# Three matrix products share one step: the expert's second product moves to the step's head

## Chip, cores, metric

One core of a Trainium2 chip. The metric is the device time of one execution in microseconds (us), lower is better.

## What is computed

An FFT convolution, then a routed expert layer, then a dense layer with softplus. Cut to what matters here (3072 tokens of 256 channels go to each batch, 8 batches, 8 experts with a capacity of 768 tokens each; tokens that no expert keeps are zero):

```python
y   = irfft(rfft(x, axis=1) * F, axis=1)          # tokens, 256 channels
e   = argmax(y @ w_gate)                          # one expert for each token
h   = relu(disp[e] @ w1[e])                       # 256 -> 1024
m   = gate * (h @ w2[e])                          # 1024 -> 256
hin = m @ w_in                                    # 256 -> 2048
g   = max(hin, 0) + log1p(exp(-abs(hin)))         # softplus
out = g @ w_out                                   # 2048 -> 256
```

Both factors of each of the four large products are split into a high and a low part, and three of the four partial products are summed.

## The kernel before

The work behind the convolution is cut into 16 **units** of 384 tokens of one expert (the list `units`; 8 experts by two blocks of slots). A unit goes through four products on PE, each in groups of matmuls that a method of `Unit` issues:

- `w1(j)`, j from 0 to 7 (line 542): 6 matmuls into a PSUM tile `pw`, then ACT's relu `hh` and DVE's remainder `hl`.
- `w2(j)`, j from 0 to 7 (line 559): 6 matmuls into the two PSUM tiles `py`, summed over all j. After the eighth, ACT copies `yh` and DVE makes `yl`.
- `wi(i)`, i from 0 to 15 (line 574), the product with w_in: 6 matmuls into a PSUM tile `pi`. `sp_act` follows on ACT (`ab` twice, then `ln`, lines 469, 470, 472), `sp_sum` on DVE (`g`, line 477), and two steps later `sp_split` (ACT's `gh`, POOL's `gl`, lines 394 and 395).
- `wo(i)` (line 597), the product with w_out: 9 matmuls into three PSUM tiles `po`, summed over all i.

When a unit's sixteenth `wo` is done, `take` (line 604) copies its three `po` tiles to `ot` on DVE, and three stores on POOL (line 609) write them out. `tr_x` (line 531) turns a unit's tokens by transposes on PE into a tile `pt`. Weights of experts come by DMA as `ws`, and `split_w` makes `w1h`, `w2h` on ACT and `w1l`, `w2l` on POOL.

PSUM tiles come from pools that go round: `psa` has three buffers, and `pi`, `pw` and `pt` take the next one in turn; `psy` has two, both for the `py` of one unit; `pso` has three, all for the `po` of one unit. A tile that takes a buffer waits until the last reader of the tile before in it is done: a `pi` waits for the `g`, `hl` or `xl` that read its buffer last, and the first `wo` of a unit for the `take` of the unit before.

The order of all instructions is written by hand (a manual schedule, every engine in program order). Each call is entered by `ev(t, rank, ...)` at a step t, and `step(t)` issues the calls of one step sorted by rank, so the ranks say who comes first within a step:

```python
WI, SP, WO, SUM, W2, W1, TAKE, TR, AHEAD = range(9)
```

Unit v has its `wi` in steps 16v to 16v + 15, its `wo` four steps after each, and its `take` in step 16v + 19. From the third unit on, with b = 16(v - 2):

```python
ev(b + 2 * j - 3 if v > 1 else 8 * v - 19 + j, W1, u.w1, j)
ev(b + 2 * j if v > 1 else 8 * v - 16 + j, W2, u.w2, j)
```

So an even step from 0 to 222 has `wi`, `wo`, `w2`; an odd one to 219 has `wi`, `wo`, `w1`. The last steps have `wi` and `wo` alone. Transposes (`tr_x`, rank TR) stand at the end of the odd steps b - 7 and b - 5. Steps before 0 belong to the convolution and to the first two units' `w1` and `w2`, and no `wi` is in them. In steps up to 19 the conversion of w_in and w_out (`split_res`, lines 449 to 465, on DVE and ACT) still runs. From step 50 on come the first stores, with those of units 0, 1 and 2 in steps 50, 52 and 54, while `late_scatter` (line 815, POOL) goes on to step 67.

Of the kernel before, what the change touches and what calls it, by code (L numbers as in the profile page):

```python
# [95 lines left out]
def body(tc, cap, x, ff, fx, wg, w1, w2, win, wout, m1, m2, m4, small, out):  # L96
# [552 lines left out]
    with tc.manual_schedule():  # L649
# [53 lines left out]
                fn(*args)  # L703

        units = [Unit(e, r + e * UNIT) for r in [hi, *range(0, hi, region)] for e in range(E)]
        WI, SP, WO, SUM, W2, W1, TAKE, TR, AHEAD = range(9)
        T1, T2, S2, GG, S4, GATE, S3, X1, ON = range(-9, 0)


# [277 lines left out]
```

## Time and profile before

| | |
|---|---|
| median of three runs | 1119.17 us (1118.44 to 1120.66) |
| the profiled execution's own time | 1115.93 us |
| its span, first to last instruction | 1114.1 us |
| mean granted TensorE clock | 0.987 of full speed |
| PE busy (matmuls) | 1056.2 us, 95% |
| PEld busy (weight loads) | 1000.0 us, 90% |
| ACT, POOL, DVE busy | 828.5, 597.2, 502.3 us |

The profile is of one execution. PE is TensorE's matmuls and PEld its weight loads, which run beside them; DVE is VectorE, ACT ScalarE, POOL GpSimd. A matmul's shown duration overlaps with the next one's, so what a matmul costs is read from one start to the next. A row names a line of the kernel, the tile written, `<-`, the tiles read. Brackets at a row's end give the idle time before it and what ended that.

### The profile page before, as it was taken

How to read it: one execution, taken by the hardware profiler on the slowest of the kernel's cores; microseconds unless marked ns; L12 is line 12 of the kernel's file. 1: busy time of each engine (PE TensorE's matmuls, PEld its weight loads, DVE VectorE, ACT ScalarE, POOL GpSimd, SP SyncE). 2: the span in 40 equal slices, each digit the busy share in tenths (PEclk: the TensorE clock that was granted, in tenths of full speed). 3: DMA queues.
4: the chain of work that ended last, by engine and by line, in shares of the span. 5: the costliest groups of instructions: out<-in, count | busy, mean ns of one | idle time of the engine just before them, and what ended most of it. 6: DMA issues, size and time to landing. Idle time of an engine off the chain costs nothing.

```text
span 1114.1 us, 19249 instructions
## 1 busy us (share of the span) xinstructions
PE 1056.2 (95%) x7040; PEld 1000.0 (90%) x7040; DVE 502.3 (45%) x1001; ACT 828.5 (74%) x1689; POOL 597.2 (54%) x590
## 2 busy tenths in 40 slices
PE   9989999778889999999999999999999999999996
PEld 7978877468778999999999999999999999999996
DVE  3757586388998743323233333333323333232221
ACT  5547665555878787777888787878877877777884
POOL 1313837534446566786554655555555555554554
PEclk9999999979999999999999999999999999999999
DMA  9942403765533156444332333332112111100000
GB/s 276 284 116 66 113 23 85 195 165 168 153 99 96 55 179 225 139 139 131 106 126 76 132 105 115 110 105 85 53 53 62 53 53 55 60 11 6 16 15 18
DMA packets 102777, 114.88 MB, mean 103 GB/s; under 512 B 12397, under 2 KB 89666, under 8 KB 102673
## 3 DMA queue, kind: packets, MB, share of 16 engines
q1 hardware_dynamic: 95760, 100.90, 30.5%
q0 software_dynamic: 6912, 12.65, 3.6%
q8 instruction: 57, 0.93, 0.4%
q14 instruction: 48, 0.39, 0.1%
HBM read 66.20 MB, written 50.48 MB: 105 GB/s over the span
## 4 chain that ended last, share of the span: by engine, by line
PE 79%; DVE 9%; DMA 3%; issue 3%; POOL 2%; ACT 2%; SPq 0%; POOLq 0%; DVEq 0%; ACTq 0%
PE po L597 23%; PE pi L574 23%; PE py L559 10%; PE pw L542 10%; PE p L204 3%; PE p L286 3%; PE p L221 2%; PE p L244 2%; DMA disp<-yt,ix 1%; PE p L251 1%; DVE wr L451 1%; PE p L211 1%; DVE whb L459 1%; DVE wtop L461 1%; DVE g L477 1%
## 5 line engine op out<-in xcount | busy, mean ns | idle before, releaser
L395 POOL TENSOR_TENSOR gl<-g,gh 128x384 fp32r<-128x384 f32 x256 | 260.7, 1019 | 190.9 <-ACT gh L394 161.2
L477 DVE SCALAR_TENSOR_TENSOR g<-pi,ln 128x384 f32<-128x384 f32 x256 | 142.5, 557 | 463.6 <-ACT ln L472 454.8
L597 PE MATMUL po<-woh,gh 128*128 128x256 f32 x768 | 218.0, 284 | 8.9 <-ACT ab L469 7.9
L597 PE MATMUL po<-woh,gl 128*128 128x256 f32 x768 | 216.9, 282 | 1.0 <-POOL gl L395 1.0
L597 PE MATMUL po<-wol,gh 128*128 128x256 f32 x768 | 216.7, 282 | 0.0
L469 ACT ACTIVATE ab<-pi 128x384 f32<-128x384 f32 x256 | 125.8, 491 | 83.1 <-PE pi L574 69.4
L574 PE MATMUL pi<-yh,wih 128*128 128x384 f32 x512 | 175.8, 343 | 9.5 <-DVE g L477 9.4
L574 PE MATMUL pi<-yh,wil 128*128 128x384 f32 x512 | 173.0, 338 | 0.0
L574 PE MATMUL pi<-yl,wih 128*128 128x384 f32 x512 | 172.5, 337 | 0.0
L597 PEld LDWEIGHTS po<-woh,gh 128*128 128x128 f32 x768 | 144.9, 189 | 14.5 <-ACT ab L469 12.0
L597 PEld LDWEIGHTS po<-woh,gl 128*128 128x128 f32 x768 | 145.3, 189 | 1.3 <-POOL gl L395 1.3
L597 PEld LDWEIGHTS po<-wol,gh 128*128 128x128 f32 x768 | 145.5, 189 | 0.0
L470 ACT ACTIVATE ab<-ab 128x384 f32<-128x384 f32 (+1 forms) x257 | 134.9, 525 | 8.1
L472 ACT ACTIVATE ln<-ab 128x384 f32<-128x384 f32 (+1 forms) x257 | 134.8, 525 | 8.1
L395 POOL TENSOR_TENSOR w1l<-ws,w1h 128x512 fp32r<-128x512 f32 x64 | 84.0, 1312 | 94.8 <-ACT w1h L394 91.6
L395 POOL TENSOR_TENSOR w2l<-ws,w2h 128x512 fp32r<-128x512 f32 x64 | 84.2, 1316 | 88.6 <-ACT w2h L394 59.7
L394 ACT CAST gh<-g 128x384 fp32r<-128x384 f32 x256 | 129.7, 507 | 0.3 <-DVE g L477 0.3
L546 ACT ACTIVATE hh<-pw 128x384 fp32r<-128x384 f32 x128 | 62.7, 490 | 71.9 <-PE pw L542 71.9
L574 PEld LDWEIGHTS pi<-yh,wih 128*128 128x128 f32 x512 | 96.6, 189 | 15.3 <-DVE g L477 12.0
L574 PEld LDWEIGHTS pi<-yl,wih 128*128 128x128 f32 x512 | 96.7, 189 | 0.0
L574 PEld LDWEIGHTS pi<-yh,wil 128*128 128x128 f32 x512 | 96.5, 188 | 0.0
L542 PE MATMUL pw<-xl,w1h 128*128 128x384 f32 x256 | 88.6, 346 | 4.0 <-DVE xl L533 4.0
(139 smaller groups left out, 2062.9 us busy)
## 6 DMA issues: line engine op xcount, KB each, us to landing
ws<-in_w_dram SPq DMA_DIRECT2D x128, 256.0 KB, 3.0
out_dram<-cr SPq DMA_DIRECT2D x48, 512.0 KB, 3.9
xt<-in_x_dram SPq DMA_DIRECT2D x20, 384.0 KB, 4.2
disp<-pf SPq DMA_DIRECT2D x12, 516.0 KB, 8.8
xd<-disp SPq DMA_DIRECT2D x48, 129.0 KB, 3.1
wst<-in_win_dram SPq DMA_DIRECT2D x16, 256.0 KB, 4.4
wst<-in_wout_dram SPq DMA_DIRECT2D x16, 256.0 KB, 3.0
lt<-parked SPq DMA_DIRECT2D x32, 96.8 KB, 2.0
```

Of the source, the lines that this page charges most:

```text
L204: nc.tensor.matmul(ps[:, i], lhsT=xt[:, 4 * (g % 2) + i], rhs=self.m1s, start=True, stop=True)
L394: nc.scalar.copy(dst_hi, src)
L395: nc.gpsimd.tensor_tensor(out=dst_lo, in0=src, in1=dst_hi.bitcast(F32), op=ALU.subtract)
L469: nc.scalar.activation(out=ab[:, :n], in_=h, func=ACTF.Abs)
L470: nc.scalar.activation(out=ab[:, :n], in_=ab[:, :n], func=ACTF.Exp, scale=-1.0)
L472: nc.scalar.activation(out=ln[:, :n], in_=ab[:, :n], func=ACTF.Ln, bias=1.0)
L477: nc.vector.scalar_tensor_tensor(out=g[:, :n], in0=h, scalar=0.0, in1=ln[:, :n], op0=ALU.max, op1=ALU.add)
L542: nc.tensor.matmul(ps, lhsT=a[:, k, fs], rhs=b[:, k], start=(n == 0), stop=(n == 5))
L546: nc.scalar.activation(out=hh, in_=ps, func=ACTF.Relu)
L559: nc.tensor.matmul(self.py[d], lhsT=a[:, j % 2, ds], rhs=b, start=(j == 0 and n == 0), stop=(j == 7 and n == 2))
L574: nc.tensor.matmul(self.pi, lhsT=a[i][:, k], rhs=b[:, k], start=(n == 0), stop=(n == 5))
L597: nc.tensor.matmul(self.po[t], lhsT=a[:, ts], rhs=b[:, i], start=(i == 0 and n == 0), stop=(i == KI - 1 and n == 2))
```

## The change

The order of the ranks: W2 goes from the fifth place to the first. Nothing is added or taken away.

```diff
-        WI, SP, WO, SUM, W2, W1, TAKE, TR, AHEAD = range(9)
+        W2, WI, SP, WO, SUM, W1, TAKE, TR, AHEAD = range(9)
```

The calls of the convolution have negative ranks and stand ahead of both. In steps before 0 there is nothing of rank WI to SUM, so the order there stays as it was.

PE around the change of a unit, from the last matmul of step 19 (`pw`) into step 20, in which the second unit's first `po` stands. Before:

```order
L542 MATMUL pw_4290<-xh_3756,w1l_3931 128x384
L574 MATMUL pi_4310<-yh_3226,wih4_2258 128x384
L574 MATMUL pi_4310<-yl_3227,wih4_2258 128x384
L574 MATMUL pi_4310<-yh_3226,wil4_2274 128x384
L574 MATMUL pi_4310<-yh_3226,wih4_2258 128x384
L574 MATMUL pi_4310<-yl_3227,wih4_2258 128x384
L574 MATMUL pi_4310<-yh_3226,wil4_2274 128x384
L597 MATMUL po_4326<-woh_2865,gh_4228 128x256
```

and of the change:

```order
L542 MATMUL pw_4290<-xh_3756,w1l_3931 128x384
L559 MATMUL py_4121<-hh_4210,w2h_4046 128x384
L559 MATMUL py_4121<-hl_4211,w2h_4046 128x384
L559 MATMUL py_4121<-hh_4210,w2l_4047 128x384
L559 MATMUL py_4122<-hh_4210,w2h_4046 128x384
L559 MATMUL py_4122<-hl_4211,w2h_4046 128x384
L559 MATMUL py_4122<-hh_4210,w2l_4047 128x384
L574 MATMUL pi_4316<-yh_3226,wih4_2258 128x384
L574 MATMUL pi_4316<-yl_3227,wih4_2258 128x384
L574 MATMUL pi_4316<-yh_3226,wil4_2274 128x384
```

Between `pw` and the unit's first `po` there were the six matmuls of `pi`; now there are the six of `py` and the six of `pi`.

PE behind the transposes of step 9 (the last of them, `pt`), where step 10 begins. Before:

```order
L531 MATMUL pt_3758<-sm_72,xd_3289 128x128
L574 MATMUL pi_3781<-yh_2974,wih10_2264 128x384
L574 MATMUL pi_3781<-yl_2975,wih10_2264 128x384
L574 MATMUL pi_3781<-yh_2974,wil10_2280 128x384
L574 MATMUL pi_3781<-yh_2974,wih10_2264 128x384
```

and of the change:

```order
L531 MATMUL pt_3758<-sm_72,xd_3289 128x128
L559 MATMUL py_3257<-hh_3642,w2h_3368 128x384
L559 MATMUL py_3257<-hl_3643,w2h_3368 128x384
L559 MATMUL py_3257<-hh_3642,w2l_3369 128x384
L559 MATMUL py_3258<-hh_3642,w2h_3368 128x384
L559 MATMUL py_3258<-hl_3643,w2h_3368 128x384
L559 MATMUL py_3258<-hh_3642,w2l_3369 128x384
L574 MATMUL pi_3787<-yh_2974,wih10_2264 128x384
```

The `pi` that followed the transposes at once now has a `py` group ahead of it.

ACT in step 14, where the third unit's eighth `w2` is followed by the copies `yh`. Before:

```order
L394 CAST gh_4014<-g_3922 128x384
L469 ACTIVATE ab_4018<-pi_4007 128x384
L470 ACTIVATE ab_4018<-ab_4018 128x384
L472 ACTIVATE ln_4021<-ab_4018 128x384
L565 CAST yh_4040<-py_3271 128x384
L565 CAST yh_4040<-py_3272 128x384
L394 CAST w2h_4046<-ws_3588 128x512
```

and of the change:

```order
L565 CAST yh_4013<-py_3257 128x384
L565 CAST yh_4013<-py_3258 128x384
L394 CAST gh_4026<-g_3928 128x384
L469 ACTIVATE ab_4030<-pi_4019 128x384
L470 ACTIVATE ab_4030<-ab_4030 128x384
L472 ACTIVATE ln_4033<-ab_4030 128x384
L394 CAST w2h_4046<-ws_3588 128x512
```

The two `yh` went from behind the softplus to ahead of it, once for each unit; DVE's `yl` went ahead of `g` in the same way. In the other even steps the order on ACT and DVE is as it was, and the order on POOL and of SP's DMAs is the same throughout.

## Rows read from the trace of the kernel before

**Rows 1.** The page, part 1: busy time of the engines over the span.
```profile
PE 1056.2 (95%) x7040; PEld 1000.0 (90%) x7040; DVE 502.3 (45%) x1001; ACT 828.5 (74%) x1689; POOL 597.2 (54%) x590
```

**Rows 2.** Windows: PE, PEld, DVE, ACT, POOL busy us (instructions); PEclk, DMA share, GB/s.
```profile
284.60:363.00 78.40, 67.69 (x405) 63.75 (x404) 72.22 (x154) 65.59 (x148) 41.47 (x38) 0.96 0.40 115
521.50:574.00 52.50, 51.95 (x345) 51.29 (x344) 16.47 (x35) 41.95 (x87) 29.98 (x28) 1.00 0.32 107
1035.00:1111.00 76.00, 67.61 (x482) 66.81 (x480) 20.29 (x40) 59.00 (x122) 41.23 (x41) 0.99 0.05 17
```

**Rows 3.** Chain that ended last, steps 16 to 17: start us, us, line and matmuls.
```profile
404.59 1.05 PE py L559 x6
405.64 1.04 PE pi L574 x6
406.68 1.07 PE po L597 x9
```

**Rows 4.** Waits of PE, 200 to 400 us, then to the end: total, times, longest.
```profile
PE po L597 <- DVE ot L604: 0.5, 1, 0.5
...
PE po L597 <- ACT ab L469: 7.9, 14, 0.7
PE po L597 <- POOL gl L395: 1.0, 1, 1.0
```

**Rows 5.** Timeline at a unit change (step 36): ACT, PE and DVE.
```profile
415.16 0.49 ACT L546 ACTIVATE hh<-pw 128x384 fp32r<-128x384 f32 x1 [0.51 <-PE pw L542]
415.82 0.34 PE L574 MATMUL pi<-yh,wil 128*128 128x384 f32 x1
416.15 1.08 DVE L604 COPY ot<-po 128x256 f32<-128x256 f32 x3
...
416.71 0.36 PE L597 MATMUL po<-woh,gh 128*128 128x256 f32 x1 [0.55 <-ACT ab L469]
416.91 0.28 PE L597 MATMUL po<-wol,gh 128*128 128x256 f32 x1
```

**Rows 6.** Timeline after a transpose: before pi (434, 967 us) and before py (275 us).
```profile
434.50 0.56 DVE L477 SCALAR_TENSOR_TENSOR g<-pi,ln 128x384 f32<-128x384 f32 x1 [2.60 <-ACT ln L472]
...
434.72 0.49 PE L531 MATMUL pt<-sm,xd 128*128 128x128 f32 x3
...
435.12 0.45 PE L574 MATMUL pi<-yh,wih 128*128 128x384 f32 x1
...
275.38 0.49 PE L531 MATMUL pt<-sm,xd 128*128 128x128 f32 x3
...
275.63 0.42 PE L559 MATMUL py<-hh,w2h 128*128 128x384 f32 x1
...
967.37 0.49 PE L531 MATMUL pt<-sm,xd 128*128 128x128 f32 x3
...
967.77 0.45 PE L574 MATMUL pi<-yh,wih 128*128 128x384 f32 x1
```

**Rows 7.** Timeline of POOL's burst: its first instruction, and PE's wait at its end.
```profile
464.45 1.29 POOL L395 TENSOR_TENSOR w2l<-ws,w2h 128x512 fp32r<-128x512 f32 x1 [1.25 <-ACT w2h L394]
...
486.84 0.39 PE L597 MATMUL po<-woh,gl 128*128 128x256 f32 x1 [1.05 <-POOL gl L395]
```

**Rows 8.** Timeline of the first steps: PE and DVE.
```profile
286.52 0.44 PE L559 MATMUL py<-hh,w2h 128*128 128x384 f32 x1 [0.70 <-DVE yl L566]
...
290.39 0.55 DVE L477 SCALAR_TENSOR_TENSOR g<-pi,ln 128x384 f32<-128x384 f32 x1
...
324.29 0.69 PE L574 MATMUL pi<-yh,wih 128*128 128x384 f32 x1 [1.90 <-DVE g L477]
```

**Rows 9.** Window at the half clock, columns as in Rows 2.
```profile
324.40:327.30 2.90, 2.90 (x11) 2.90 (x12) 2.65 (x8) 0.65 (x2) 0.73 (x1) 0.50 0.65 176
```

**Rows 10.** L451 on DVE: its group, and minimum, median, maximum, 284 to 363 us.
```profile
L451 DVE TENSOR_SCALAR wr<-wst 128x256 uint32<-128x256 uint32 x18 | 10.8, 599 | 0.0
...
L451 DVE TENSOR_SCALAR wr<-wst x18: 278/288/1394, 285.1 to 351.0; 128x256 uint32<-128x256 uint32 x18
```

## The prediction

> **What bounds the kernel now.** I began with the page: PE has matmuls for 95% of the span, no other engine over 74% [rows 1]. The windows then separate three stages. From 284 to 363 us (steps 0 to 19) DVE is busy for 72.2 of 78.4 us and PE for 67.7: DVE bounds it, since it still converts w_in and w_out. In the middle, 522 to 574 us, PE has 51.95 of 52.5 us and nothing else is near. From 1035 us on no `w1` or `w2` is left [rows 2]. So in the middle only PE's waits can be won.
>
> The chain shows the rhythm there: a `py` group takes 1.05 us, a `pi` group 1.04, a `po` group 1.07 (a `pw` group as much as `py`), so a step has 3.16 us of matmuls and an unbroken chain of them [rows 3]. PE's waits show what breaks it: the first `po` of a unit waits 14 times after 400 us and once before, and one `po` waits for POOL [rows 4]. The page's releaser for the 14 is ACT's `ab`; the timeline says otherwise. `ab` has nothing that `po` needs, while DVE's three copies `ot`, which free the `po` buffers, begin at 416.15, 0.36 us each, and `po` starts at 416.71, when the first is out [rows 5]. The wait is for `take`.
>
> The idle time in the row, 0.55 us, is not the price. From start to start, 415.82 to 416.71 is 0.89 us where a matmul of `pi` needs 0.17 (1.04 / 6), and the next one comes 0.20 later where `po` needs 0.12 (1.07 / 9) [rows 3, 5]: 0.72 + 0.08 = **0.80 us** for each wait.
>
> A smaller wait hides behind the transposes. DVE's `g` ends at 435.06 and `pi` starts at 435.12, 0.40 us after `pt`; a `py` that follows `pt` and waits for nothing starts 0.25 us after it [rows 6]. So `pi`, whose buffer that `g` must free, loses **0.15 us**. From 388 to 968 us there are 23 such places, the last one again at 0.40 [rows 6].
>
> **The change, part by part.** No instruction is added; DMAs, and the order on POOL and SP, stay. In each of 112 even steps 1.05 us of `py` matmuls go from behind `wo` to ahead of `wi`.
>
> *The take waits.* The first `po` of a unit now has `py` and `pi` ahead of it, 2.09 us instead of 1.04. The copies don't move with it: they stand behind DVE's `hl`, `hl` behind ACT's `hh`, and `hh` behind `pw` of the odd step, which stays where it was; ACT stood idle for 0.51 us waiting for `pw` [rows 5], so it can take a softplus that ends a little later. `po` would start 1.05 us after the old place, about 417.05, 0.5 us after the first copy's end, and its second and third tile need theirs 0.36 and 0.72 us later still, as the copies come 0.36 apart. The wait goes. It goes where the step has a `w2`: of the 14, two lie in the tail without `w2`, and one (469 us) I leave to POOL below, which leaves 11 x 0.80 = 8.8; the one before 400 us (0.5 idle) gives 0.7. **-9.5 us**, between 0 (the copies slip along) and -11.
>
> The Trainium skill, Perfetto Trace Analysis, section Optimization Strategy, speaks against this: the same gap repeating on the engine that should be saturated can mean that there is not enough SBUF or PSUM for the next tile. By that, no reordering helps and this term is 0. The rows show the three buffers of `po` short by 0.56 us a unit, less than the 1.05 that comes in between; so I keep the term.
>
> *The waits behind transposes.* `py` follows `pt` and reads nothing that is late; `pi` comes 1.05 us later, when `g` has long ended. 23 x 0.15 = **-3.4 us**. At 381 us a longer wait of this kind stands; its `g` hangs on ACT, which will run a `pi` later, so I count nothing for it (at best -1.2).
>
> *POOL's burst.* `pi` of even steps comes 1.05 us later within the step, so everything behind its softplus on ACT does too: `w2h`, and POOL's `w2l`, which waits for it. That is harmless while POOL has gaps, but from 464.45 on the stores of three units follow each other there, and at 486.84 PE waits 1.05 us for `gl` [rows 7]. If the burst begins 1.05 us later, it ends so: I take **+1.0 us**, and nothing for the take wait inside it, which would only lengthen this one. Ends: -0.8 (the burst has slack) and +2.
>
> *The first steps.* In step 0, `py` waits for `yl` until 286.52; now `pi` is behind it, 2.9 us later than before. But DVE reaches the first `g` only at 290.39 and had no idle time before it [rows 8]: the softplus fits in, and some 0.4 us is lost in the next step. Against it: at 324.29 `pi` starts after 1.90 us of idle and its matmul lasts 0.69 us [rows 8]; the window shows a granted clock of 0.50 there, the lower level, 1.2 GHz [rows 9]. With `py` in front, about half of that idle time is filled; should the clock stay up, the `pi` group ends about 1 us sooner, and DVE waits for it. PE's other gains here are worth nothing, as DVE sets the pace. **-0.8 us**, but with wide ends, -6 to +6, since DVE's times themselves scatter: the 18 of line 451 take 288 ns at the median and 599 in the mean, and up to 1394 [rows 10]. That is 18 x 0.311 = 5.6 us on one line of six such lines.
>
> *Once a unit* the copies `yh` go ahead of the softplus on ACT. `py` ends with the matmul at 1.05 us of the step, `yh` is out 1 us later, about when `pi` is (2.09): at worst 0.2 us on ACT, which at that place had idle time; 0.
>
> The sum: -9.5 - 3.4 + 1.0 - 0.8 = **-12.7 us**. The profiled execution's 1115.93 becomes 1103.2. It lies 3.2 us under the median of the runs, so against 1119.17 I forecast **1106.4 us**, and call its own case 1101 to 1111 (all ends but those of take).
>
> **The rivals.**
>
> *The wait moves.* The copies slip, because ACT or DVE have become later in the odd step by as much as PE, or another buffer is short. For it: the pairs of `pi` now stand 2.1 and 4.2 us apart instead of 3.16, and ACT's four operations for one (about 2 us) just fit the short one. Against: 0.51 us of idle time before `hh`. Then the take term is 0, and with it the loss in the burst changes little: 1119.2 - 3.4 + 1.0 - 0.8 = 1116; half of it gives 1111. Chance 0.15.
>
> *The first stage gains more.* If fewer of DVE's conversions are stretched and no clock falls, 6 us more: 1100, at the far end 1096. For it: 5.6 us on one line alone. Against: nothing in the change aims at it. Chance 0.12.
>
> *Slower: DVE and POOL collide more in the first stage.* Line 451 takes 278 ns alone and up to 1394 when something holds it. POOL works for 41.5 of the 78.4 us [rows 2]. The Trainium skill, SBUF — State Buffer, section Who interferes with whom, has the cause: a DVE operation with two SBUF inputs or in a two-port mode and a GpSimd operation exclude each other for a whole instruction. No row here shows which instruction held which. The shift of 1.05 us changes how the two fall together. Each stretched operation costs up to 1.1 us (1394 - 288 ns); it takes 14 more of them to eat up the 12.7 + 2.2 us, and from there the kernel is slower, 1122 us and beyond. Against: the six lines have 18 or 19 such operations each in the stage, POOL's time bounds what they can lose, and nothing drives all of them one way. Chance 0.05.
>
> The rest, 0.03, is no effect. That the matmuls do not move is excluded by the order shown above.
>
> **How the numbers follow.** The forecast's case has 0.65, and 1106.4 is its time. 1099 to 1114.5 leaves out a part of the first-stage gain (0.05), the larger part of the moved wait (0.08) and the slower case (0.05). 0.2% is 2.2 us, about what a measurement can tell from no change: 1117 and 1121.4. Below 1117 lie the forecast, the larger gain and most of the moved wait: 0.90 faster. Same 0.05, slower 0.05.
>
> **What would show it.** Right: the first `po` of a unit without idle time up to 1000 us, with both in the tail still there; transposes followed by `py` after 0.25 us; a middle window with PE over 99%; POOL's wait near 485 us longer, about 2 us or split over two `po`. Wrong: waits of `po` of 0.3 us and more at the unit changes with `ot` starting later after `pw`; new waits of `pi` for `g`, or of `py`, in the middle; DVE busy in the first stage for 5 us more or less than 72.

## The result, and the profile after

The changed kernel took **1108.02 us** in the median of six runs (1105.56 to 1111.81), the kernel before, beside it on the same chip, 1118.20 (1116.08 to 1120.66): a ratio of 0.9915, 95% interval [0.9892, 0.9938]. The profiled execution took 1107.81 us with a span of 1106.0, 8.1 less than that of before.

The page, part 1, and three windows of the changed kernel, columns as in [rows 2] (they answer to rows 1 and 2, moved by what the stages before them gained or lost):

```profile
PE 1051.1 (95%) x7040; PEld 999.9 (90%) x7040; DVE 502.0 (45%) x1001; ACT 818.6 (74%) x1689; POOL 597.1 (54%) x590
```

```profile
288.80:366.00 77.20, 65.88 (x397) 61.80 (x397) 71.23 (x151) 64.18 (x145) 40.45 (x37) 0.98 0.40 117
523.50:576.00 52.50, 52.50 (x352) 52.43 (x351) 16.42 (x35) 42.07 (x89) 31.34 (x30) 1.00 0.33 106
1027.00:1103.00 76.00, 67.76 (x483) 66.96 (x481) 20.41 (x40) 59.16 (x122) 41.20 (x41) 0.98 0.05 18
```

The middle window has no idle time left: PE 52.50 of 52.50 us, where it had 51.95 [rows 2]. In the last window nothing changed; in the first PE has a little more idle time, and DVE is the busiest engine as before.

PE's waits in the changed kernel from 380 us to the end (total us, times, longest):

```profile
PE po L597 <- POOL gl L395: 1.7, 2, 1.5
PE po L597 <- ACT ab L469: 1.3, 2, 0.7
PE pi L574 <- DVE g L477: 1.0, 1, 1.0
PE po L597 <- DVE ot L604: 0.8, 2, 0.6
```

Of the 14 waits of a unit's first `po` [rows 4] the two of the tail remain, 1.3 us, and the one among the stores (0.8, now on two `po`). The `pi` row is the wait at 381 us, still there. The change of a unit at step 36, which answers to [rows 5], ACT, DVE and PE:

```profile
418.62 0.49 ACT L546 ACTIVATE hh<-pw 128x384 fp32r<-128x384 f32 x1 [0.21 <-PE pw L542]
419.62 1.07 DVE L604 COPY ot<-po 128x256 f32<-128x256 f32 x3
420.33 0.34 PE L574 MATMUL pi<-yh,wil 128*128 128x384 f32 x1
420.50 0.28 PE L597 MATMUL po<-woh,gh 128*128 128x256 f32 x1
420.62 0.28 PE L597 MATMUL po<-wol,gh 128*128 128x256 f32 x1
```

The copies start 1.00 us after `hh`, as before (0.99), so they did not slip; `po` now stands 0.17 us behind the last `pi` and the next matmul 0.12 behind it, the bare cadence. It starts 0.88 us after the first copy; before, 0.56 was enough. What was used up is ACT's slack: its idle time ahead of `hh` shrank from 0.51 to 0.21 us. The transposes at step 41 (they answer to [rows 6]):

```profile
437.40 0.49 PE L531 MATMUL pt<-sm,xd 128*128 128x128 f32 x3
437.65 0.42 PE L559 MATMUL py<-hh,w2h 128*128 128x384 f32 x1
```

`py` follows after 0.25 us, where `pi` came after 0.40.

**Where the time came from.** I cut the span at the first `pi` of odd steps; "0" is the end of the last `pw` ahead of step 0 (its last matmul's start + 0.17 us), and "end" is the end of the last matmul, behind which every span has another 9.3 to 10.8 us. The table holds the eleven experiments too, which the next section tells one by one; all but the first two rows were profiled on other chips than the first pair.

| us | start of 0 | 0-20 | 21-38 | 39-50 | 51-66 | 67-130 | 131-218 | 219-end | 0-end |
|---|---|---|---|---|---|---|---|---|---|
| before | 284.61 | 79.77 | 60.86 | 38.94 | 54.46 | 209.48 | 287.96 | 87.85 | 819.32 |
| change | 288.77 | 79.40 | 59.73 | 38.62 | 54.84 | 205.13 | 281.72 | 87.86 | 807.30 |
| e1 | 311.54 | 79.11 | 60.08 | 38.94 | 54.47 | 206.40 | 283.28 | 87.85 | 810.13 |
| e2 | 309.67 | 80.66 | 59.67 | 38.60 | 53.78 | 208.18 | 286.29 | 87.85 | 815.03 |
| e3 | 304.60 | 79.75 | 60.07 | 38.95 | 55.40 | 206.33 | 283.20 | 86.04 | 809.74 |
| e4 (change) | 306.92 | 79.34 | 59.73 | 38.62 | 54.81 | 205.13 | 281.73 | 87.85 | 807.21 |
| e5 | 308.59 | 79.29 | 59.76 | 38.63 | 54.81 | 205.14 | 281.72 | 86.07 | 805.42 |
| e6 | 304.21 | 79.29 | 59.75 | 38.63 | 54.63 | 205.13 | 281.72 | 87.87 | 807.02 |
| e7 | 311.46 | 78.72 | 59.75 | 38.63 | 51.29 | 205.13 | 281.72 | 86.06 | 801.30 |
| e8 | 309.88 | 79.10 | 59.75 | 38.63 | 54.80 | 205.13 | 281.72 | 87.84 | 806.97 |
| e9 | 305.65 | 77.98 | 59.74 | 38.62 | 55.96 | 205.14 | 281.72 | 87.85 | 807.01 |
| e10 | 310.39 | 77.92 | 59.74 | 38.62 | 51.29 | 205.13 | 281.72 | 86.05 | 800.47 |
| e11 (before) | 309.83 | 79.79 | 60.85 | 38.93 | 54.46 | 209.46 | 287.91 | 87.83 | 819.23 |

From step 0 on the change takes 12.0 us off; 10.6 of them lie in steps 67 to 218. Ahead of step 0, where the order is the same, its one profile is 4.2 us longer than that of before; the start of step 0 differs by 7 us between executions on the other chips, so this says nothing of the change. From step 21 on, the same order gives the same stage within 0.1 us, on every chip (before and e11, change and e4), so tenths can be read there from one profile. The exception is 51-66, where stores are about: e9, with the change's order there, took 1.12 us more. Steps 0 to 20 need a finer cut, which comes with e8 to e11.

### The profile page after: what moved, and what is told of

Read it like the earlier page. It is cut to its first block, busy times and chain, and to the rows that moved or that the text cites. A ratio compares the mean times of both kernels' runs of the same rounds, so it can differ in the third digit from the quotient of the medians.

```text
span 1106.0 us, 19249 instructions
## 1 busy us (share of the span) xinstructions
PE 1051.1 (95%) x7040; PEld 999.9 (90%) x7040; DVE 502.0 (45%) x1001; ACT 818.6 (74%) x1689; POOL 597.1 (54%) x590
## 4 chain that ended last, share of the span: by engine, by line
PE 78%; DVE 7%; POOL 4%; DMA 3%; ACT 3%; issue 3%; SPq 0%; POOLq 0%; DVEq 0%; ACTq 0%
PE po L597 22%; PE pi L574 22%; PE pw L542 10%; PE py L559 10%; PE p L204 3%; PE p L286 3%; PE p L221 2%; PE p L244 2%; PE p L251 1%; DMA disp<-yt,ix 1%; PE p L211 1%; DVE wr L451 1%; POOL z L234 1%; DMA yt<-in_x_dram 1%; DVE wtop L461 1%
## 5 line engine op out<-in xcount | busy, mean ns | idle before, releaser
L559 PE MATMUL py<-hh,w2h 128*128 128x384 f32 x256 | 89.5, 350 | 3.7 <-DVE yl L566 3.7
L559 PE MATMUL py<-hl,w2h 128*128 128x384 f32 x256 | 87.0, 340 | 5.6 <-DVE hl L547 5.6
```

Source lines behind the costliest of these rows:

```text
L559: nc.tensor.matmul(self.py[d], lhsT=a[:, j % 2, ds], rhs=b, start=(j == 0 and n == 0), stop=(j == 7 and n == 2))
```

## The experiments

Each ratio is to the kernel before on the same chip, with its 95% interval. Four kernels first, to part the terms of the sum.

**e1: the take waits alone.** `w2` goes to the head only in the step of each unit that starts its first `po` (from step 20 on); the rank -0.5 stands ahead of `WI`, which is 0.

```diff
-                ev(b + 2 * j if v > 1 else 8 * v - 16 + j, W2, u.w2, j)
+                ev(b + 2 * j if v > 1 else 8 * v - 16 + j, -0.5 if v > 1 and b + 2 * j >= 20 and j == 2 else W2, u.w2, j)
```

> w2 stands at the head of the step only in the steps in which a unit's first po stands (20, 36, ... 212). Theory (py covers the wait for take, 0.80 us each): 11 x 0.80 + 0.7 = 9.5 us less than before, ratio about 0.9915; no idle time before the first po of a unit up to 1000 us, the waits behind transposes as before, and POOL's wait near 485 us longer by 0.8 (1.05 to about 1.85 us), since PE comes to it earlier. Rival 1 (the copies slip along, the wait only moves): the same time as before. Rival 2 (the gain comes from the new rhythm of all even steps, not from this place): under 2 us less.

Measured: 1130.98 against 1139.12 us, ratio 0.9920 [0.9894, 0.9947]. Steps 67 to 130 lost 3.08 us over four changes of a unit, steps 131 to 218 lost 4.68 over six: **0.77 and 0.78 us each**, where 0.80 was predicted. Its waits from 380 us on:

```profile
PE pi L574 <- DVE g L477: 2.0, 3, 1.2
PE po L597 <- POOL gl L395: 1.8, 2, 1.5
PE po L597 <- ACT ab L469: 1.3, 2, 0.7
```

The wait among the stores went too (steps 51 and 52: 6.49 instead of 7.53 us), and PE's waits for `gl` behind it grew by as much (steps 55 to 58: 15.82 instead of 14.80): nothing won in that stage, 54.47 against 54.46.

**e2: the transposes alone.** The same line with `j in (5, 6)`: `w2` at the head only in the two steps that follow transposes.

> w2 stands at the head only in the two even steps of a unit that follow its transposes. Theory (py covers the wait for g, 0.15 us each): 23 x 0.15 = 3.4 us less than before, ratio 0.997, waits of po at the unit changes as before. Rival 1 (what is lost behind transposes is the switch from transposes to matmuls and stays): no change. Rival 2 (rhythm of all even steps): no change either, as only 2 of 8 move.

Measured: 1132.74 us, ratio 0.9948 [0.9927, 0.9969]. Steps 67 to 130 lost 1.30 us over eight places, 131 to 218 lost 1.67 over ten: **0.16 and 0.17 each** (predicted 0.15). With e1 this adds up to the change: 4.38 and 6.35 us, against its 4.35 and 6.24. Its waits for the take stay:

```profile
PE po L597 <- ACT ab L469: 6.8, 12, 0.6
PE po L597 <- DVE ot L604: 1.7, 3, 0.7
PE po L597 <- POOL gl L395: 1.1, 1, 1.1
PE pi L574 <- DVE g L477: 0.6, 1, 0.6
```

Two stages differ from the sum of e1 and e2. In 51-66, e2 has 53.78 and the change 54.84 us; only the change begins POOL's burst later, and I put the **1.06 us** between them down to that. It is the difference of two profiles, in the one stage where the same order also gave another time (e9). And in steps 25 and 26 (7.09 us in e2, 7.93 in the change, 8.10 before) the longer wait at 381 us nearly goes when the even steps before it keep their order, but not in the change.

**e3: the copies earlier instead.** PE's order is that of before; the copies `ot` go ahead of the `g` of the same step on DVE.

```diff
-        WI, SP, WO, SUM, W2, W1, TAKE, TR, AHEAD = range(9)
+        WI, SP, WO, TAKE, SUM, W2, W1, TR, AHEAD = range(9)
```

> The order on PE stays that of before; in its step take goes ahead of sp_sum on DVE, so the three copies no longer stand behind g and hl. Theory (the wait is for take): the wait goes at all unit changes, those of the tail too: 9.5 + 2 x 0.8 = 11 us less than before, ratio 0.990. Rival 2 (rhythm of the even steps): no change, as PE's order is the same. By the page's releaser (ab): no change.

Measured: 1128.74 us, ratio 0.9910 [0.9884, 0.9936]; from step 0 on 9.6 us less. Its waits from 380 us on, and one change of a unit:

```profile
PE po L597 <- issue: 2.1, 1, 2.1
PE pi L574 <- DVE g L477: 1.2, 1, 1.2
```

```profile
433.37 1.14 DVE L604 COPY ot<-po 128x256 f32<-128x256 f32 x3 [1.25 <-PE po L597]
434.73 0.56 DVE L477 SCALAR_TENSOR_TENSOR g<-pi,ln 128x384 f32<-128x384 f32 x1 [0.22 <-ACT ln L472]
```

All waits of `po` at unit changes are gone, in the tail as well (86.04 instead of 87.85). This shows the cause directly: the releaser was the copy, late because it stood behind `g` and `hl` on DVE (in the tail behind `g` alone), and not `ab`, which the page names. The price is a new wait in the burst (55.40): there a copy waits 4.29 us for a free `ot`, with `g` behind it, and the first `po` of step 52 waits 2.1 us, for which the view names no releaser.

**e4: the change again**, on the chip of e1 to e3.

> The change once more. From step 0 on its first profile was 12.0 us shorter than that of before, while the stage ahead of step 0, whose order is the same, took 4.2 us more. If that stage's time only scatters from run to run, this profile puts step 0 within 2 us of 285 us and the ratio is 0.989 to 0.992. If the change really lengthens it, step 0 comes near 289 us again and the ratio is 0.9915 or above.

Measured: 1126.99 us, ratio 0.9897 [0.9872, 0.9921]; every stage from 21 on within 0.03 us of the first profile. Its step 0 starts at 306.92 us, near neither of the two times expected.

**e5, e6: what could be added.** e5 is the change with `TAKE` ahead of `SUM` (`W2, WI, SP, WO, TAKE, SUM, W1, TR, AHEAD`); e6 is the change with the stores of the first units five steps apart:

```diff
-            ev(max(16 * v + 21, 50 + 2 * v), AHEAD, u.store, "out")
+            ev(max(16 * v + 21, 50 + 5 * v), AHEAD, u.store, "out")
```

> The change, and take ahead of sp_sum on DVE besides. Theory (both moves cure the same wait): they don't add up. Only the two waits in the tail, which have no w2 in front, go as well: 1.7 us less than the change (steps 219 to the end 86.1 instead of 87.85 us), while the unit changes up to 1000 us give nothing more. In steps 51 to 67 up to 1 us more, as take then stands in front of g while it waits for a free ot. Together 807.2 to 806.3 us from step 0 on. Rival (two separate gains): 10 us less than the change.

> The change, with the stores of units 0, 1 and 2 in steps 50, 55 and 60 instead of 50, 52 and 54. Theory (POOL's burst sets the end of step 57, and the change starts it 1.05 us later): PE's waits for gl near step 57 (1.7 + 0.3 us) go, steps 51 to 67 take 52.8 instead of 54.8 us; the wait for ot at step 52 (1.1 us) stays, as unit 2's take needs the ot of unit 0 stored. Rival (something else holds PE there): 54 to 55 us as in the change.

Measured: e5 1125.00 against 1139.67 us, ratio 0.9874 [0.9847, 0.9900]: the tail lost 1.8 us as expected, nothing else moved. e6 1124.11 us, ratio 0.9870 [0.9839, 0.9900], but 54.63 us in 51-66 instead of the 52.8 expected: a miss. DVE's longest wait for a free `ot` in e6, and PE's behind it, from the timeline:

```profile
490.64 0.42 DVE L604 COPY ot<-po 128x256 f32<-128x256 f32 x1 [2.46 <-DMA out_dram<-ot,ids]
...
491.12 0.39 PE L597 MATMUL po<-woh,gh 128*128 128x256 f32 x1 [2.27 <-DVE ot L604]
```

The waits for `gl` went, and one for `ot` took their place. There are seven `ot` buffers; the take in step 51 needs two that hold unit 0's tiles, and their stores start only in step 50.

**e7: both, with the first store a step earlier**: e5's ranks and `max(16 * v + 21, 49 + 6 * v)`.

> The change, take ahead of sp_sum, and the stores of the first units in steps 49, 55 and 61. By the theory the tail's waits (1.7 us), POOL's burst (2.0 us) and, with the first store a step sooner, most of the wait for ot (1.1 us) go: 807.2 - 4.5 = about 803 us from step 0 on, 4 us less than the change and 0.986 of the kernel before. If ot still waits in step 51, take holds up DVE and 2 us of it are lost.

Measured: 1123.80 us, ratio 0.9853 [0.9824, 0.9883]; 51-66 fell to 51.29 us and the whole from step 0 on to 801.30. Neither `gl` nor `ot` makes PE wait after 380 us.

**e8 to e11: the first steps.** The cut of steps 0 to 20, in us (the change, and its repeat e4, have `w2` at the head in all even ones, before and e11 in none):

| | 0 | 1-8 | 9-10 | 11-14 | 15-18 | 19-20 | sum |
|---|---|---|---|---|---|---|---|
| before | 3.06 | 29.81 | 11.50 | 13.81 | 14.54 | 7.05 | 79.77 |
| e11 (before) | 3.07 | 29.84 | 11.36 | 13.92 | 14.55 | 7.05 | 79.79 |
| change | 4.13 | 29.24 | 9.77 | 14.78 | 14.49 | 6.99 | 79.40 |
| e4 (change) | 4.10 | 29.18 | 9.77 | 14.80 | 14.50 | 6.99 | 79.34 |
| e8 | 4.04 | 29.19 | 9.77 | 15.25 | 14.55 | 6.30 | 79.10 |
| e9 | 3.07 | 28.85 | 9.81 | 14.78 | 14.48 | 6.99 | 77.98 |
| e10 | 3.06 | 28.88 | 9.77 | 15.32 | 14.58 | 6.31 | 77.92 |

The take wait of step 20 gave only 0.06 us in the change, though it is gone. In step 0 and from step 11 on, PE's waits in the changed kernel show two things that take time back:

```profile
290.68 0.45 PE L559 MATMUL py<-hh,w2h 128*128 128x384 f32 x1 [1.73 <-DVE yl L566]
...
333.51 0.39 PE L597 MATMUL po<-woh,gh 128*128 128x256 f32 x1 [0.40 <-ACT woh L465]
...
348.47 0.39 PE L597 MATMUL po<-woh,gh 128*128 128x256 f32 x1 [0.56 <-ACT woh L465]
355.81 0.38 PE L597 MATMUL po<-woh,gh 128*128 128x256 f32 x1 [0.74 <-ACT woh L465]
362.79 0.39 PE L597 MATMUL po<-woh,gh 128*128 128x256 f32 x1 [0.39 <-ACT woh L465]
```

ACT ahead of the last of these, in the changed kernel:

```profile
361.40 0.53 ACT L472 ACTIVATE ln<-ab 128x384 f32<-128x384 f32 x1
361.83 0.60 ACT L394 CAST w2h<-ws 128x512 fp32r<-128x512 f32 x1
362.34 0.40 ACT L465 CAST woh<-whb 128x256 fp32r<-128x256 f32 x1
```

and at the same place before:

```profile
356.49 0.53 ACT L472 ACTIVATE ln<-ab 128x384 f32<-128x384 f32 x1
356.93 0.60 ACT L394 CAST w2h<-ws 128x512 fp32r<-128x512 f32 x1
357.44 0.40 ACT L465 CAST woh<-whb 128x256 fp32r<-128x256 f32 x1
```

The first `pi` of step 19 starts at 361.18 us in the changed kernel and at 357.33 before. So ACT's cast of `woh`, which stands behind the softplus and `w2h` of step 18, starts 1.16 us after it instead of 0.11: it is 1.05 us later against PE, and step 19's `po` needs it. Three edits of the `w2` line test this; in e8 the condition is

```diff
-                ev(b + 2 * j if v > 1 else 8 * v - 16 + j, W2, u.w2, j)
+                ev(b + 2 * j if v > 1 else 8 * v - 16 + j, W1 - 0.5 if v > 1 and b + 2 * j in (12, 14, 16, 18) else W2, u.w2, j)
```

which is the old place, behind `SUM`; e9 has `(0,)` there, and e10 is e7 with `(0, 12, 14, 16, 18)`. e11 is the kernel before.

> The change, but w2 stands at its old place in steps 12, 14, 16 and 18. In the change's first stage po of steps 11, 13, 15, 17 and 19 waits 0.39 to 0.74 us for woh, which ACT casts behind the softplus and the w2h of the even step, 1.05 us later than before. Theory A (these waits took back the take wait of step 20 and part of what steps 9 to 11 gained): with the old place the waits of po for woh fall from 2.5 us in five to 0.9 us or less in one or two, and steps 0 to 20 take 78.1 us instead of the 79.3 of the change. Rival B (DVE sets the pace there, the waits of PE for woh only stand where PE would wait for DVE): the waits go but pi waits longer for g, and the stage stays at 79.3. From step 21 on all as in the change (727.9 us) by both.

> The change, but w2 stands at its old place in step 0 alone. In the change the first py waits 1.73 us for yl with pi behind it, and steps 0 to 1 take 4.1 us instead of 3.06. Theory A (this is a real loss, since DVE has 8.5 us of work in the first 10 us): steps 0 to 20 take 78.3 us instead of 79.3. Rival B (DVE's work catches up, pi of the next steps waits for g as much longer): 79.3. The wait of py for yl falls from 1.7 to 0.7 us by both.

> The best version so far (the change, take ahead of sum, stores spread) with w2 at its old place in steps 0, 12, 14, 16 and 18. Theory A: steps 0 to 20 take 76.9 us or less, all of it from step 0 on 799 us. Rival B: 78.7 to 79.3 and 801.3.

> The kernel before, for a second profile of it. If the stages from step 21 on are a matter of the order alone, each comes within 0.1 us of the first profile (60.86, 38.94, 54.46, 209.48, 287.96, 87.85 us); steps 0 to 20 within 1 us of 79.8, with the lower clock granted in steps 9 to 10 as in all four profiles with the old order there; and the start of step 0 differs by several us.

*e8* measured 1128.69 against 1138.73 us, ratio 0.9905 [0.9868, 0.9941]; steps 0 to 20 took 79.10 us, nearer to rival B's 79.3 than to A's 78.1, but each theory holds at a place of its own. Its waits from step 0 to step 21:

```profile
PE pi L574 <- DVE g L477: 7.7, 7, 2.0
PE py L559 <- DVE yl L566: 1.7, 1, 1.7
PE pt L531 <- DVE g L477: 1.7, 1, 1.7
PE po L597 <- ACT woh L465: 0.8, 2, 0.5
```

The waits for `woh` fell from 2.5 us in five (the change) to 0.8 in two. Steps 19 and 20 gained 0.69 us (6.30 after 6.99), the full price of step 20's take wait, and steps 13 and 14 gained 0.58 (6.41 after 6.99): A. But `pi` of step 12 now waits 1.26 us for `g` where it waited 0.21 in the change, and steps 11 and 12 lost 1.05 (8.84 after 7.79): there DVE sets the pace, B. That wait in e8, and in the changed kernel:

```profile
358.45 0.44 PE L574 MATMUL pi<-yh,wih 128*128 128x384 f32 x1 [1.26 <-DVE g L477]
...
337.49 0.45 PE L574 MATMUL pi<-yh,wih 128*128 128x384 f32 x1 [0.21 <-DVE g L477]
```

e1, in which these steps have the order of before and step 20 has `w2` at its head, needs 6.31 us for steps 19 and 20 as well.

*e9* measured 1125.72 us, ratio 0.9888 [0.9855, 0.9921]. The wait for `yl` in step 0 fell to 0.7 us, and steps 0 to 20 to 77.98: 1.06 us came back in step 0, theory A. The 0.36 behind it is not clear of scatter: e7, with the change's order there, took 28.61 us in steps 1 to 8, less than e9's 28.85. So `w2` at the head of step 0 costs 1.06 us; whether more belongs to it is open.

*e10* measured **1120.64 us, ratio 0.9842 [0.9817, 0.9867]**, the lowest ratio of all, though its interval overlaps e7's; from step 0 on 800.47 us, 1.5 more than the 799 of theory A, 1.1 of it in steps 11 and 12, which lose it as in e8. From 380 us on the view of PE's waits holds only the one `pi` of 1.0.

*e11* agrees with the first profile in every stage within 0.05 us, with step 0 starting 25 us later. Its two windows from the first `pi` of steps 9 and 11 (PEclk is the third number from the end), then those of the changed kernel:

```profile
342.74:354.10 11.36, 8.42 (x47) 7.87 (x47) 9.88 (x24) 7.84 (x18) 4.52 (x6) 0.85 0.39 118
354.10:368.02 13.92, 13.34 (x88) 12.92 (x88) 13.58 (x27) 12.15 (x29) 8.89 (x8) 1.00 0.32 88
```

```profile
322.14:331.91 9.77, 7.28 (x46) 6.65 (x47) 9.49 (x22) 7.22 (x17) 5.23 (x5) 1.00 0.45 130
331.91:346.69 14.78, 13.78 (x89) 12.79 (x88) 14.20 (x29) 13.27 (x32) 8.42 (x8) 1.00 0.33 97
```

In steps 9 and 10 the clock falls in all five profiles with the old order there (mean 0.73 to 0.85, 11.36 to 12.74 us) and in none of the eight with `w2` at the head (1.00, 9.75 to 9.81).

## Why the prediction was right, and where it was not

The forecast was 12.7 us off the time of before; from step 0 on it was 12.0, and on a median of 1119.17 the interval of the ratio makes 6.9 to 12.1. So the forecast lies 0.6 us beyond that interval; the one of e4, the same change on another chip, makes 8.8 to 14.3. Term by term:

| term | predicted | measured, from |
|---|---|---|
| 11 take waits after 400 us | -8.8 | -8.55 (0.79 at step 36 in the change, 3.08 + 4.68 in e1) |
| take wait before 400 us (step 20) | -0.7 | -0.06, steps 19-20 |
| 23 transposes | -3.4 | -4.2 (e2: 0.20 + 0.34 + 0.68 + 1.30 + 1.67) |
| POOL's burst | +1.0 | +1.06 (change against e2) |
| first steps, 0 to 18 | -0.8 | -0.31 |
| wait at 381 us | 0 | -0.17, steps 25-26 |
| sum | -12.7 | -12.2; -12.0 from end to end |

The sum came within half a microsecond in part because misses cancel: step 20 and the first steps gave 1.1 us less than forecast, the transposes 0.8 more. The range "1101 to 1111" of the forecast's own case does not follow from the ends that are named with it: those of the burst and of the first steps make 1099 to 1114. The measured 1108.0 lies in either.

**Right, by its own steps.** The take waits went because `po` moved and the copies did not, priced from start to start; the row's idle time, 0.55 us, would have given 6.1 for the 11 instead of 8.55. The Trainium skill (Perfetto Trace Analysis, Optimization Strategy) says that such a regular gap can mean too few buffers; that no reordering would help then was the prediction's own conclusion from it, and the runs refute that: e1 removed the gap by PE's order and e3 by DVE's, both with the buffers of before. Whether more `po` buffers would have done it too, no run tried. The burst did what was said: POOL's `w2l` of step 50, at 464.45 us [rows 7], now starts at 467.85. That is 3.40 later, while the `pi` of the odd steps around it stand 2.34 later, so it lies 1.06 us later within its step. POOL's first instruction and PE's waits among the stores in the changed kernel:

```profile
467.85 1.29 POOL L395 TENSOR_TENSOR w2l<-ws,w2h 128x512 fp32r<-128x512 f32 x1 [1.95 <-ACT w2h L394]
...
472.88 0.39 PE L597 MATMUL po<-woh,gh 128*128 128x256 f32 x1 [0.58 <-DVE ot L604]
473.71 0.39 PE L597 MATMUL po<-woh,gh 128*128 128x256 f32 x1 [0.21 <-DVE ot L604]
482.13 0.38 PE L597 MATMUL po<-woh,gl 128*128 128x256 f32 x1 [0.16 <-POOL gl L395]
490.24 0.39 PE L597 MATMUL po<-woh,gl 128*128 128x256 f32 x1 [1.53 <-POOL gl L395]
```

The wait near 485 us grew from 1.05 to 1.53 and split, as the text had it, and the take wait inside gave nothing. For the transposes one of the 23 was worth 0.5 us instead of 0.15 (steps 57 and 58 took 8.48 us before, 7.98 in e2), the others 0.17; it lies in POOL's burst, and why it gave more stays open. The rival "the wait moves" does not hold at the unit changes after 400 us, where ACT's slack of 0.51 us covered what it had to, with 0.21 left.

**The step that failed** is "the one before 400 us (0.5 idle) gives 0.7". The wait went and 0.06 us came of it, because another took its place one step ahead: `po` of step 19 waits for `woh`. The prediction said that everything behind the softplus of even steps comes 1.05 us later on ACT, and followed `w2h` and POOL's `w2l`; it did not follow the cast of `woh`, which stands on the same queue while w_in and w_out are still converted. e8 shows it: with that wait gone, the 0.69 us appear; in e1 it is 0.74 (6.31 us after 7.05). This is the rival "the wait moves", at a place where it was not looked for.

**Mis-sized inside the first steps.** "Some 0.4 us is lost in the next step" was 1.07 in step 0 itself, and e9 got 1.06 of it back. DVE had no idle time before its first `g` [rows 8], but in the changed kernel it waits there, for the softplus of the later `pi`:

```profile
294.74 0.56 DVE L477 SCALAR_TENSOR_TENSOR g<-pi,ln 128x384 f32<-128x384 f32 x1 [1.21 <-ACT ln L472]
```

The clock did stay up where the text said, at [rows 8, 9]: steps 9 and 10 gained 1.73 us, where about 1 was put down. Steps 11 to 14 gave back 0.97 of it, and steps 1 to 8 gained 0.57 that was not forecast and whose cause stays open. The four add to -0.26, with -0.05 in 15 to 18, for -0.8: that it came so near is luck, for it is not the sum that was written. Of DVE against POOL as a cause of stretched conversions, which the text weighed as a rival, no run settled anything: DVE is busy for 73.14 us in steps 0 to 20 before and for 72.55 in the change.

## What to carry to other kernels

When an in-order engine waits for a buffer, look for work that is ready to go ahead of the wait, and price the wait from start to start against the cadence of a place without one. Then follow every instruction that becomes later on each queue, not only those of the moved step: here one cast that nobody had counted took back a whole term in a stage bound by another engine. A reorder that helps the steady part may hurt its first steps; there it can be left out (e9, e10).

## What the runs showed of the hardware

In steps 3 to 6, where DVE set the pace, a fall of the clock cost no time. It fell there in ten of the thirteen profiles, not in e4, e6 and e8. Of e8:

```profile
319.81:335.40 15.59, 12.67 (x75) 11.62 (x75) 15.18 (x32) 13.64 (x32) 7.99 (x8) 1.00 0.42 121
```

and of the changed kernel:

```profile
298.78:314.44 15.66, 13.61 (x75) 13.10 (x75) 15.25 (x32) 13.71 (x32) 7.93 (x8) 0.89 0.42 120
```

PE was busy for 0.94 us more at the lower clock, and the stretch took 0.07 us more, for DVE had 15.2 of it to do in either. In steps 9 and 10 a lower clock and a longer time go together with the same order: 11.36 to 11.50 us at a mean of 0.85 in before, e1 and e11, 12.66 and 12.74 at 0.73 and 0.74 in e3 and e2. DVE stood idle for 1.48 of the 11.36 us in e11 and for 0.28 of the 9.77 in the change, so in e11 it did not set the pace there alone. How much of the 1.6 us between these two is the clock and how much the order, no run parts.

The stage ahead of step 0, the same in all kernels here, took 284.6 and 288.8 us on one chip and 304.2 to 311.5 on the others. For a part of it the clock is the row that differs: from 100 to 200 us it is 1.00 in the first profile of before, with 705 matmuls done, and 0.90 in e11, with 595. It also goes with the start of step 0 on one and the same chip: 0.90 and 309.67 us in e2, 0.93 and 306.92 in e4, 0.97 and 304.60 in e3. Why it falls there was not tried. A second open point is when stores land: e9 has the change's order in the burst, but 55.96 us for 54.8, with a wait of `po` for `ot` of 1.6 us in step 52 and one of 1.0 ahead of it.
